# The same steps of an attention and feed-forward kernel in another written-out order, with other engines for some of the elementwise steps

## The chip, the cores and the metric

The kernel runs on one core of a Trainium2 chip. The metric is the device time of one execution in microseconds (us), taken as the median of several runs. The core has five instruction queues that matter here: TensorE (PE; its weight loads are shown apart as PEld), VectorE (DVE), ScalarE (ACT), GpSimd (POOL) and SyncE (SP), which issues most of the DMAs. Each engine works through its own queue in order and waits on semaphores for the others.

## The reference

Two blocks follow each other. The attention maps each row of q and k (4 batches, 4 heads, 1088 positions, 32 dimensions) to 64 features, products of two sketches of 8, and then applies the linear form of attention. Its output is laid out as 4352 tokens of 128 numbers and goes through a multiplicative feed-forward network with 1024 inner features.

```python
def phi(x):
    a = np.einsum('rd,bhsd->bhsr', S1, x)
    b = np.einsum('rd,bhsd->bhsr', S2, x)
    return np.einsum('bhsi,bhsj->bhsij', a, b).reshape(*x.shape[:-1], r * r)
q_p, k_p = (phi(q), phi(k))
kv = np.einsum('bhsf,bhsd->bhfd', k_p, v)
z = np.sum(k_p, axis=2)
num = np.einsum('bhsf,bhfd->bhsd', q_p, kv)
den = np.einsum('bhsf,bhf->bhs', q_p, z)[..., None] + 1e-06
x = (num / den)              # transposed to (4352, 128)
h = (x @ w1) * (x @ w2) @ w3
out = h @ w_out
```

The denominator can come near zero, so the kernel computes it with numbers split into a leading part and a rest. The weights and sketches arrive as 64-bit floats and are turned into fp32 on the chip.

## The kernel before, in words

The program is cut into 1179 named steps, each a function that emits the instructions of one small piece of work. A string named ORDER (lines 75 to 143) lists the names, and the loop at line 1892 calls the steps in that order. Lines 1900 to 1904 then chain the instructions of each engine in the order in which they were emitted, so the string fixes every engine's queue.

```python
for name in ORDER.split():
    n = len(traced)
    steps.pop(name)()
```

The names have a prefix for the piece and a suffix for the operation:

- `w0` to `w10`: the weights. `.load` fetches 64-bit words, `.c` and `.m` (ScalarE) and `.j` (VectorE) and `.a` (GpSimd) turn them into fp32 (lines 422 to 504). `f0` to `f7` fold w3 with w_out, so that one product replaces two (`.m`, line 534).
- `k0` to `k3`: the keys of a batch. `.lead` and `.rest` split k into a leading part and a rest (lines 641 to 651), `.gram0` to `.gram4` form the Gram matrix (128*32 tiles of TensorE, line 659), `.Gm`, `.Gt`, `.Ga`, `.Gb`, `.T0`, `.Ta`, `.N0`, `.Na`, `.N1`, `.Nb` are a chain between TensorE and VectorE that turns it into the denominator's matrix (lines 847 to 937), and `.Nh`, `.Nf`, `.Nr` put that into block form (lines 939 to 954). `.kp0` and `.kp1` make the features of k (line 677), `.kv0` to `.kv3` and `.kvr` multiply them with v (line 769), `.kqt` and `.kq` turn the result. `kr0` and `kr1` are the last 64 positions of two batches each.
- `q0` to `q6` and `qr`: tiles of queries. q0 and q1 have 512 positions, q2 and q3 512 in another layout (`q_wide`, line 1309), q4 and q6 1024, qr the rest. `.A0`, `.C0`, `.C1` are their products with the sketches, `.sm` to `.rc` compute the reciprocal of the denominator (`.p01`, `.p2`, `.p12` multiply leading parts and rests), `.phi` makes features, `.pt` or `.pT` transposes them, `.x` multiplies with kv and `.xT` copies the result into the tile that the network reads.
- `g0` to `g3` and `gr`: the network for one tile of tokens. For each of 8 chunks of inner features, `.a` and `.b` are products of 128*128 weights with up to 512 columns (lines 1799 and 1809), `.c` copies a out of PSUM (line 1804), `.m` multiplies it with b (VectorE, line 1815), and `.o` adds the chunk's output (line 1835, for gr `.o0` and `.o1`, line 1824).
- `h4` and `h6`: the same network for two tiles of tokens at a time with seven products instead of eight (Strassen's way, in Winograd's form). Their first products, such as `h4.0a1`, use 64*128 halves of TensorE's array (line 1673), two at a time; the second ones, `P1` to `P7`, 128*64 halves (line 1759). `.m11` and the like multiply (line 1707), `.T1` to `.T4` form sums (lines 1723 to 1742), `.k1` to `.k9` combine the outputs.
- `s`: constants; `v` and `o`: sums of weights for h4 and h6; `warm0` to `warm11`: idle products on zeros (line 255), 53 in all, which keep TensorE at work where it would stand.

Three more constants belong to the order. SLOTS (line 28) names the buffer that each tile takes, in the order of allocation. The set POOL (line 53) lists the steps whose elementwise operation runs on GpSimd instead of VectorE, through `on(name)` at line 176. The set CPV (line 65) lists the copies that run on VectorE instead of ScalarE, through `cp(name)` at line 179. Large loads are also held back so that at most four are under way (line 1898).

TensorE can work with its whole array (128*128) or with a part of its rows or columns (128*32, 128*64, 64*128, 32*32 and so on). In the trace each product shows the shape that it uses.

## Time and profile before

| what | value |
|---|---|
| runs | 245.04, 245.12, 245.30 us |
| median | 245.12 us |
| span of the profiled execution, first to last instruction | 244.1 us |
| TensorE, products | 236.2 us, 97% |
| VectorE | 206.7 us, 85% |
| GpSimd | 161.9 us, 66% |
| ScalarE | 123.5 us, 51% |
| chain that ended last | 87% TensorE, 5% DMA |

The profile shows one execution. Its busy times are unions of the instructions' spans on an engine; the ends of products are modelled, so the starts are what one compares. A row of a group gives the source line, the engine, the operation, the tile written and read, the shape, the count, and then busy time in us, the mean of one in ns, and the idle time ahead of it. A row of the timeline gives the start in us from the first instruction, the duration, and in brackets an idle time ahead of it with what ended it. "Issue" in such a bracket means that the engine waited for nothing that the profile shows. A row of the busy times by stretches gives the stretch, its length, then for each engine the busy time and the number of instructions, then the granted clock of TensorE, the DMA engines' share and GB/s.

### The profile page before, as it was taken

Reading aid. Unit: us, or ns where it says so; the run is one execution under the profiler, and the core shown is the slowest. Engines: PE = TensorE matmul, PEld = TensorE weight load, DVE = VectorE, ACT = ScalarE, POOL = GpSimd, SP = SyncE. Lnnn points to the kernel's source line nnn. Section 1 sums busy time; section 2 is a strip of 40 time slices with the busy share of each in tenths; the row PEclk is TensorE's granted clock in tenths of the full one; section 3 lists DMA queues with packets and bytes.
Section 4 is the critical chain, followed back from the end, with each engine's and each line's share of the span. In section 5 each row is a group of like instructions: output and inputs, shape, how many; then the busy total and the mean of one; then the engine's idle time right before and its main releaser. Section 6 shows DMA issues by size and latency. Waiting matters only on the chain.

```text
span 244.1 us, 6745 instructions
## 1 busy us (share of the span) xinstructions
PE 236.2 (97%) x2724; PEld 129.8 (53%) x2724; DVE 206.7 (85%) x421; ACT 123.5 (51%) x246; POOL 161.9 (66%) x203
## 2 busy tenths in 40 slices
PE   8998999899999999999999999999999999999994
PEld 5887454545545646766566444444443354463363
DVE  2876988999899998997899878498989789999792
ACT  3976957675666764593012914355651164730010
POOL 4576658344856998764583889929999425883670
PEclk9999999999999999999999999999999999999999
DMA  7959797078859897200000000360000000000054
GB/s 201 265 143 325 181 227 190 6 197 224 220 141 251 188 217 190 59 1 3 3 0 0 4 0 3 59 113 3 1 0 0 0 3 0 0 1 3 12 90 93
DMA packets 31935, 22.06 MB, mean 90 GB/s; under 512 B 21280, under 2 KB 26528, under 8 KB 31904
## 3 DMA queue, kind: packets, MB, share of 16 engines
q1 hardware_dynamic: 31360, 21.11, 35.1%
q8 instruction: 21, 0.34, 0.6%
q10 hardware_dynamic: 544, 0.52, 0.6%
q14 instruction: 10, 0.08, 0.1%
HBM read 19.40 MB, written 2.23 MB: 89 GB/s over the span
## 4 chain that ended last, share of the span: by engine, by line
PE 87%; DMA 5%; ACT 2%; POOL 2%; DVE 1%; issue 1%; POOLq 0%; SPq 0%
PE b_ps L1809 12%; PE ps_o L1835 12%; PE ps_X L1673 11%; PE a_ps L1799 11%; PE ps_o L1759 10%; PE ps_w3o L534 6%; PE ps_Y L1673 6%; PE ps_Z L1673 3%; PE ps_g L659 2%; PE ps_x L1527 2%; PE ps_ac L1374 2%; DMA qh<-in_q_dram 2%; DMA k<-in_k_dram 2%; PE ps_or L1824 2%; POOL ph L1208 1%; PE idle_ps L255 1%
## 5 line engine op out<-in xcount | busy, mean ns | idle before, releaser
L1673 PE MATMUL ps_X<-xd,wv 64*128 64x512 f32 x112 | 36.3, 593 | 0.0
L1799 PE MATMUL a_ps<-xT,w 128*128 128x512 f32 (+1 forms) x80 | 36.1, 562 | 0.0
L1809 PE MATMUL b_ps<-xT,w 128*128 128x512 f32 (+1 forms) x80 | 35.6, 555 | 0.0
L1804 ACT COPY ffa<-a_ps 128x512 f32<-128x512 f32 (+1 forms) x38 | 20.1, 540 | 29.2 <-PE a_ps L1799 26.7
L1707 POOL TENSOR_TENSOR hc<-hc 128x512 f32<-128x512 f32 x16 | 20.7, 1304 | 15.7 <-DVE hc L1685 15.5
L1835 PE MATMUL ps_o<-ab,w3o 128*128 128x512 f32 x64 | 29.6, 600 | 0.0
L1680 ACT COPY hc<-ps_X 128x512 f32<-128x512 f32 x38 | 21.3, 590 | 16.1 <-PE ps_X L1673 12.9
L1815 DVE TENSOR_TENSOR ab<-ffa,b_ps 128x512 f32<-128x512 f32 (+1 forms) x40 | 23.9, 623 | 4.9 <-PE b_ps L1809 4.1
L501 POOL TENSOR_TENSOR w3c<-w3c,cv_m 128x512 int32<-128x512 int32 x16 | 21.2, 1344 | 4.2 <-DVE w3c L495 4.1
L1673 PEld LDWEIGHTS ps_X<-xd,wv 64*128 64x128 f32 x112 | 14.9, 186 | 13.1 <-issue 10.9
L1799 PEld LDWEIGHTS a_ps<-xT,w 128*128 128x128 f32 x80 | 14.1, 189 | 13.9 <-issue 8.8
L1809 PEld LDWEIGHTS b_ps<-xT,w 128*128 128x128 f32 x80 | 14.4, 190 | 13.1 <-issue 8.1
L1673 PE MATMUL ps_Y<-xd,wv 64*128 64x512 f32 x48 | 19.7, 594 | 0.0
L1835 PEld LDWEIGHTS ps_o<-ab,w3o 128*128 128x128 f32 x64 | 11.6, 190 | 13.4 <-issue 13.0
L534 PEld LDWEIGHTS ps_w3o<-wo,w3T 128*128 128x128 f32 x128 | 15.3, 192 | 2.4 <-issue 2.4
L534 PE MATMUL ps_w3o<-wo,w3T 128*128 128x128 f32 x128 | 15.7, 276 | 0.0
L1759 PE MATMUL ps_o<-hc,w3o 128*64 128x512 f32 x32 | 15.1, 595 | 0.0
L1759 PE MATMUL ps_o<-tt,ws 128*64 128x512 f32 x32 | 13.7, 594 | 0.0
L1680 ACT COPY hc<-ps_Y 128x512 f32<-128x512 f32 x14 | 8.1, 592 | 9.7 <-PE ps_Y L1673 6.6
L263 ACT ACTIVATE cv_c<-raw 128x1024 f32<-128x1024 f32 (+1 forms) x13 | 13.0, 1014 | 0.0
L1540 ACT COPY xd<-ps_x 64x256 f32<-64x256 f32 x24 | 8.8, 367 | 7.2 <-PE ps_o L1835 6.8
L1497 POOL COPY nz<-nz 32x8 f32<-32x8 f32 x32 | 11.1, 347 | 1.4
(347 smaller groups left out, 593.0 us busy)
## 6 DMA issues: line engine op xcount, KB each, us to landing
raw<-in_moe_w_dram SPq DMA_DIRECT2D x32, 256.0 KB, 5.0
qh<-in_q_dram SPq DMA_DIRECT2D x4, 544.0 KB, 4.5
raw<-in_moe_w_dram SPq DMA_DIRECT2D x4, 512.0 KB, 5.8
out_dram<-oT SPq DMA_DIRECT2D x32, 64.0 KB, 2.0
k<-in_k_dram SPq DMA_DIRECT2D x3, 512.0 KB, 5.1
v<-in_v_dram SPq DMA_DIRECT2D x2, 512.0 KB, 6.1
kh<-in_k_dram SPq DMA_DIRECT2D x8, 128.0 KB, 3.6
raw<-in_moe_w_out_dram SPq DMA_DIRECT2D x4, 256.0 KB, 5.0
```

Source lines behind the costliest of these rows:

```text
L263: act.activation(dst, hi.bitcast(F32), ACT.Prelu, scale=2.0 ** -112, alpha=-2.0 ** 32)
L501: pool.tensor_tensor(d, d, x["m"][:, i * 512:(i + 1) * 512], ALU.add)
L534: pe.matmul(t["o"], w3T[ko][:, c], wo[:, c], start=c == 0, stop=c == NC - 1)
L1673: pe.matmul(x[bank], stat(j, u)[:, i * 128:(i + 1) * 128], rows(j, u), start=new, stop=True, tile_position=(u * 64, 0), skip_group_check=True)
L1680: cp(n(y))(x[k], x[bank])
L1707: on(f"h{g}.{i}m{k}").tensor_mul(both[0][k], both[0][k], both[1][k])
L1759: pe.matmul(acc_o[bank][half[0]:half[1]], w(i), x(i), start=n == 1, stop=n == (2 if j == 3 else 4), tile_position=(0, half[0]), skip_group ...
L1799: pe.matmul(x["a"][:, :w], w_of(0, c), xT[g][:, c0:c0 + w], start=True, stop=True)
L1804: cp(f"g{g}.{c}{su}c")(x["s"][:, :w], x["a"][:, :w])
L1809: pe.matmul(x["b"][:, :w], w_of(1, c), xT[g][:, c0:c0 + w], start=True, stop=True)
L1815: dve.tensor_mul(ab_sb[g, c][:, c0:c0 + w], x["s"][:, :w], x["b"][:, :w])
L1835: pe.matmul(o_ps[g], w3o[:, c], ab_sb[g, c], start=n == 1, stop=n == NC)
```

## The change

No function is changed and no instruction is added or taken out. The first 61 names of ORDER stay; the other 1118 are put into another order, SLOTS is rewritten to go with it, and POOL and CPV have other members. 33 steps leave POOL and 33 others enter it. Of those that leave CPV, seven are real copies (for `k2.kT1`, `k3.kT0` and `k3.kT1` the set has no effect, since their transposes always run on VectorE); 21 enter it. Parts of the diff:

```diff
 POOL = set("""
-    g4.oS g5.oS g6.oS g7.oS h4.0T1 h4.0T2 h4.0T3 h4.0m12 h4.0m22 h4.1T2 h4.1m11 h4.1m12 h4.2m11
-    h4.2m12 h4.2m22 h4.3m11 h4.s2 h4.s4 h6.0T2 h6.0m11 h6.0m12 h6.0m22 h6.1T2 h6.1T3 h6.1m11 h6.1m12
-    h6.1m22 h6.2T1 h6.2T4 h6.2m11 h6.3T3 h6.3m11 h6.s1 h6.s2 h6.s4 k0.Nf k0.Nh k0.Nr k0.kp1 k1.Nr
-    k1.kp1 k2.kp0 k2.kp1 k2.rest0 k3.kp0 k3.kp1 q0.al q0.p01 q0.phi1 q0.sca q1.al q1.bs q1.p12
-    q1.phi q1.sca q2.bs q2.p2 q2.phi0 q2.sc q2.sl q3.al q3.bs q3.p01 q3.p12 q3.p2 q3.phi0 q3.sc
-    q4.al q4.bs q4.nn q4.p01 q4.p2 q4.phi0 q4.sl q6.al q6.nn q6.p01 q6.phi1 q6.sc q6.sl qr.al qr.bs
-    qr.p12 qr.p2 s.KS s.Pp s.blk s.blkh s.low s.rest
+    g4.oS g5.oS g6.oS g7.oS h4.0T1 h4.0T2 h4.0T3 h4.0T4 h4.0m11 h4.0m22 h4.1T1 h4.1T3 h4.1m11
+    h4.1m22 h4.2T2 h4.2T4 h4.2m11 h4.3m11 h4.s2 h4.s3 h4.s4 h6.0T1 h6.0T2 h6.0T3 h6.0T4 h6.0m11
+    h6.0m12 h6.0m22 h6.1T3 h6.1T4 h6.1m12 h6.1m22 h6.2T1 h6.2T3 h6.2m11 h6.2m12 h6.2m22 h6.3m12
+    h6.s2 h6.s3 h6.s4 k0.Nh k1.kp0 k1.kp1 k2.Nr k2.kp0 k2.kp1 k3.kp1 q0.p01 q0.phi0 q0.phi1 q0.sca
+    q1.al q1.p12 q1.p2 q1.phi q1.scy q2.al q2.bs q2.p12 q2.p2 q2.phi0 q3.al q3.bs q3.p01 q3.p2 q3.sc
+    q4.al q4.bs q4.p12 q4.p2 q4.phi0 q4.phi1 q4.sc q4.sl q6.bs q6.p2 q6.phi0 q6.sl qr.al qr.p2
+    qr.phi0 qr.sc s.AR s.KS s.Pp s.blk s.blkh s.low s.rest
 """.split())
 CPV = set("""
-    g0.0c g0.1c h4.1ac h4.1ad h6.1bc h6.2ad k0.kT1 k1.kvc k2.kT1 k2.kq k3.kT0 k3.kT1 k3.kq q0.xc0
-    q0.xc1 q6.xT0 q6.xT2
+    g0.0c g0.1c g0.6c g1.3c g1.5c g2.0c g2.1c g3.0c g3.2c g3.3c g3.6c gr.2c gr.4c h4.0ac h4.1ad
+    h4.1bd h4.2bd h6.0ae h6.2be h6.3bd k0.kT1 k1.kT1 k2.kq k3.kq q4.xT1 q4.xT2 q6.xT2 q6.xT3
 """.split())
```

And the order at its start, around the Gram products of k2, and at its end:

```diff
-k1.zero s.Pm warm5 q0.l1 q0.A0 warm6 kr0.ab k0.lead1 q0.rm q0.sma q0.sta warm7 k0.kT0 v0.load v0.loadr k1.load k0.ab1
-q0.sha k0.rest1 q0.C0 k0.gram1 k0.gram2 k0.gram3 k0.gram4 k0.ab0 k0.abc1 q1.max q0.C0t q0.sla q1.l2 k1.loadr s.Pp
-k0.Gm k0.Gt k0.Ga w1.c1 k0.Gb k0.abc0 k0.T0 q1.l1 warm8 kr0.abc k0.kp1 q0.sca w1.j1 k0.Ta k0.kp0 k0.Gc w1.c0 k1.tr0
-kr1.load k2.zero k1.tr1 k1.kT1 kr0.kp warm9 k0.N0 warm10 k0.Na warm11 k0.T1 k0.kv0 k0.Tc k0.Tb k0.N1 k0.Nb k0.Nh q1.rm
...
-q1.pc0 q1.pt1 g0.1b w9.load k1.N0 s.AR q2.l1 q2.rm v3.zero q1.pc1 k1.N1 q1.x g0.6c g0.1c k1.Na k1.Nr k3.zero k2.gram0
-g0.1m k2.gram1 k2.gram2 q3.max k2.gram3 g0.0c k2.kT0 k1.Nb q1.xT k2.gram4 q3.l2 k2.ab q2.A0 q2.C0 q2.C1 q3.l1 k1.kp0
...
-h6.1P2 h6.3P6 h6.2m12 h6.2T4 h6.3T4 h6.2P7 h6.2P6 h6.3P4 h6.2P4 g4.oT h6.2P2 gr.3o1 h6.k1 gr.2o0 gr.2o1 h6.2P3 h6.k3
-g4.oS h6.k2 h6.k4 h6.0P3 gr.7o0 g4.st gr.0a gr.5b h6.k5 h6.k6 h6.3P3 h6.1P3 h6.k7 g5.oS q6.ns gr.4a gr.3o0 gr.4b gr.0c
...
+k1.zero s.Pm warm5 q0.l1 q0.A0 warm6 kr0.ab k0.lead1 q0.rm q0.sma q0.sta q0.sha k0.ab1 q0.C0 kr1.load k0.gram1 k0.abc1
+k0.rest1 q0.sla v0.loadr s.Pp k0.kT0 k0.ab0 kr1.tr k0.kp1 q1.max v0.load s.KS k1.loadr warm11 k0.gram2 k0.abc0
+k0.gram3 k0.gram4 q0.C0t k0.kp0 kr1.kT k0.kv0 k0.Gm q1.l2 k0.kv3 kr0.abc k1.load k0.kv1 k0.Gt k0.Ga k0.T0 w1.c0 q0.sca
+q0.al k0.Gc k0.Gb k0.Ta q0.phi0 k0.T1 k1.tr1 q1.l1 w0.load k0.N0 k1.max q1.rm kr1.ab w9.load kr0.kp k0.Na k0.Tc q0.pt0
+w1.c1 k0.Nh k0.Tb q0.A1 k1.kT1 q1.load q1.A0 q0.smy q1.sm k0.N1 k0.Nb k0.kv2 q0.sty q1.C0 k0.Nf q0.phi1 k1.lead0 w1.j1
...
+k3.zero k1.Gt k1.Ga q1.de g0.5c k0.kq s.AR g0.4b k2.lead0 g0.7c g0.0a q1.rc k1.Gb k2.rest0 q1.bs k2.kT1 w0.a0 k1.T0
+k2.gram0 k1.T1 k1.Ta k2.gram1 k2.gram2 q2.max k2.gram3 k2.gram4 q3.l2 k1.N0 g0.5m g0.4m g0.0c g0.3a k2.Gm g0.2c q1.phi
+w9.j w9.m g0.7b q3.l1 q1.pt1 k1.Tc k1.Tb q1.pt0 g0.7m q2.l2 g0.1a k3.loadr w2.load k3.load k1.kp0 q1.pc0 k1.Na v1.zero
+s.RC v1.load k1.Nr g0.1b g0.6m g0.1c g0.1m q1.pc1 k1.N1 g0.3c q1.x q2.l1 q1.restT k2.ab k1.Nb q2.A0 q1.xT q2.rm q2.C0
...
+h6.2P1 h6.3P5 h6.2T3 h6.1P2 gr.2m h6.3P3 q6.ns h6.3T4 h6.3P2 h6.k1 h6.2P7 h6.3P6 h6.1P5 h6.2P6 h6.3P7 h6.1P3 h6.k2
+h6.k3 h6.2P4 h6.3P4 h6.k4 h6.k5 h6.k7 h6.k6 h6.0P3 h6.k8 gr.2o1 g6.oT gr.0a gr.0c gr.4b gr.3a gr.2o0 gr.6b gr.5b h6.k9
+gr.7o1 gr.4m g4.oS g7.oT gr.3c gr.0b g6.oS gr.1o0 gr.1o1 gr.5m gr.4o1 gr.4o0 gr.7o0 g4.st gr.0m gr.6m gr.3b g7.oS
+g6.st gr.3m gr.5o0 gr.0o1 gr.0o0 g7.st gr.6o1 gr.3o1 gr.6o0 gr.5o1 gr.3o0 gr.oT0 gr.oT1 gr.st1
```

In the new order warm7, warm8, warm9 and warm10 stand far behind the start: warm9 ahead of `qr.max`, warm8 ahead of `g3.4c`, warm7 ahead of `g0.7o` and warm10 ahead of `g3.1o`.

More of the change, by code (lines that the diff above doesn't have):

```diff
@@ L83 @@
-q0.al k0.Nf q0.phi0 q0.phi1 q0.A1 q0.smy w1.m1 k1.max q0.sty q0.shy k0.kv3 k0.kv1 k0.kv2 q0.sly s.KS k0.kvr kr1.tr
-k0.kvm w1.m0 kr1.kT q0.p01 q1.C0 q1.C1 q0.C1 k0.kzt k2.loadr q0.pt0 q0.C1t q0.scy q0.p2 k0.kz q0.pt1 k0.kvc kr1.ab
-k0.kqt q0.p12 q0.dn q0.de q0.rc w1.j0 q0.pc0 q0.pc1 q0.x0 k1.kT0 q0.x1 q0.xs0 q0.xs1 q0.xt0 w1.a0 q1.A0 k2.load
-w0.load k1.lead0 q0.xc0 q0.xc1 k0.kq w1.a1 k2.max q0.xt1 k1.ab q0.xT0 q0.xT1 g0.4a q1.load g0.5a q1.sm w0.m1 q1.st
-q1.Ct g0.4c g0.4b q1.sh q1.sl k1.rest0 g0.7b w0.c1 g0.7a k1.abt w0.j1 k1.gram0 w0.c0 s.RC q1.scy k1.gram1 kh2.load
@@ new lines @@
+w1.m1 k1.tr0 q0.de k0.kz q0.x0 w1.m0 q0.rc q1.st q0.pc1 q0.xs0 q1.Ct k2.zero q0.xs1 q1.sh q0.xc0 q0.x1 q0.xt0 q1.sl
+k1.kT0 q0.xc1 kr1.abc q0.xT0 q0.xt1 w0.m0 q1.sca q0.xT1 k1.rest0 w1.a0 k0.kqt k2.loadr w1.a1 k2.load w0.m1 k1.ab g0.4a
+w0.c1 g0.6a q1.p01 q1.al g0.4c g0.5b q1.scy g0.5a k1.gram0 g0.6c q2.tr k1.gram1 k1.gram2 k1.abt k1.gram3 q1.p2 q1.p12
+kh2.load w0.c0 w0.j1 w5.load w0.a1 k1.gram4 q1.dn q3.tr k1.Gm w9.c g0.7a k1.Gc g0.6b g0.2a k2.kT0 k2.max w0.j0 q3.max
+k3.zero k1.Gt k1.Ga q1.de g0.5c k0.kq s.AR g0.4b k2.lead0 g0.7c g0.0a q1.rc k1.Gb k2.rest0 q1.bs k2.kT1 w0.a0 k1.T0
```

122 lines of the change are left out of this document (59 added, 63 removed).

## The prediction

> **What bounds the kernel now.** I read the page first: busy shares, then the busy time by stretches, then the timeline of TensorE around its few gaps.
>
> ```profile
> span 244.1 us, 6745 instructions
> PE 236.2 (97%) x2724; PEld 129.8 (53%) x2724; DVE 206.7 (85%) x421; ACT 123.5 (51%) x246; POOL 161.9 (66%) x203
> ```
>
> ```profile
> 9.50:27.40 17.90, 16.25 (x446) 13.33 (x446) 13.67 (x44) 14.26 (x32) 11.76 (x19) 1.00 0.75 231
> 27.40:156.10 128.70, 127.30 (x1822) 70.92 (x1822) 113.64 (x243) 71.31 (x138) 90.14 (x84) 1.00 0.43 107
> 156.10:240.50 84.40, 84.40 (x400) 39.33 (x396) 74.82 (x121) 33.03 (x63) 56.56 (x69) 1.00 0.14 23
> 242.50:244.10 1.60, 0.00 (x0) 0.00 (x0) 0.00 (x0) 0.00 (x0) 0.00 (x0) 0.71 0.08 27
> ```
>
> In these rows stand the stretch, its length, and the busy time of PE, PEld, DVE, ACT and POOL, then the granted clock. From 27.4 us, where the first large product g0.4a starts, TensorE is busy for 127.3 of 128.7 us, and from 156.1 us without a break. So the time after 27.4 us is what TensorE has to execute, and only three things in it can move: the cost of a change of tile shape, the gaps of about 1.4 us, and the extra instructions that the order puts there. Before 27.4 us TensorE is padded with idle products (warm steps), and the chain through VectorE, ScalarE and GpSimd sets the pace.
>
> The span is 244.1 us and the median of the runs 245.12, so 1.0 us lies outside the span; I keep it as it is and make the sum on the span. About 0.2% (0.5 us) is what a measurement can tell from no change.
>
> **Cost of a change of shape.** One fp32 product is two passes of 512 columns.
>
> ```profile
> 57.02 0.59 PE L1809 MATMUL b_ps<-xT,w 128*128 128x512 f32 x1
> 57.45 1.02 PE L1799 MATMUL a_ps<-xT,w 128*128 128x512 f32 x2
> 58.40 1.10 PE L769 MATMUL ps_kv<-kp,v 128*32 128x64 f32 x64
> ...
> 59.77 1.12 PE L1799 MATMUL a_ps<-xT,w 128*128 128x512 f32 x2
> 60.74 0.59 PE L1809 MATMUL b_ps<-xT,w 128*128 128x512 f32 x1
> ```
>
> By the starts, a pass takes 0.43 us (57.02 to 57.45). The two passes before the change to 128*32 take 0.95 instead of 0.86, so leaving costs 0.09. The two after the return to 128*128 take 0.97, so entering costs another 0.11.
>
> I gave each TensorE step of the two orders its shape from the trace and counted neighbours that differ: 75 in the old order, 64 in the new. Up to g0.4a it is 22 against 18, from there to the first h4 product 42 against 39 (entries into the full array 16 against 14), from there to the end 11 against 7.
>
> ```profile
> 230.33 0.59 PE L1759 MATMUL ps_o<-tt,w3o 128*64 128x512 f32 x1
> ...
> 230.86 0.94 PE L1824 MATMUL ps_or<-w3o,ab 128*128 128x128 f32 x6
> 231.72 1.08 PE L1759 MATMUL ps_o<-hc,ws 128*64 128x512 f32 x4
> 232.73 0.49 PE L1824 MATMUL ps_or<-w3o,ab 128*128 128x128 f32 x2
> 233.06 0.60 PE L1799 MATMUL a_ps<-xT,w 128*128 128x256 f32 x2
> ...
> 234.01 1.08 PE L1759 MATMUL ps_o<-hc,ws 128*64 128x512 f32 x4
> 235.02 0.70 PE L1799 MATMUL a_ps<-xT,w 128*128 128x256 f32 x2
> ```
>
> The four changes that go at the end are two islands of P3 products among the remainder's (231.72 and 234.01); the new order joins them to the long run of P products. From 230.86 to 235.02 pass 4.16 us. The passes alone need 6 x 0.11, twice 0.86 for the islands (four passes on two halves of the array, two at a time), 2 x 0.11 and 0.86 for 0a and 5b: 3.46. That is 0.70 for four changes: **-0.7 us**. In the middle, three fewer at 0.09 and two entries fewer at 0.11: **-0.5 us**. The four at the start I count at nothing: they lie beside the chain that sets the first 27 us.
>
> **The gaps.** Three times the weight loads stop while nothing of the profile holds them.
>
> ```profile
> 14.27 0.11 PEld L659 LDWEIGHTS ps_g<-k,kk 128*32 128x32 f32 x1 [0.54 <-issue]
> ```
>
> ```profile
> 20.35 0.15 PEld L769 LDWEIGHTS ps_kv<-kp,v 128*32 128x32 f32 x7 [1.06 <-issue]
> ```
>
> ```profile
> 46.99 0.11 PEld L659 LDWEIGHTS ps_g<-k,kk 128*32 128x32 f32 x1 [1.27 <-issue]
> ```
>
> ```profile
> 0.00:14.26 14.26, 12.59 (x221) 10.28 (x221) 7.93 (x24) 9.53 (x24) 7.66 (x41) 1.00 0.84 236
> 0.00:20.34 20.34, 17.76 (x345) 14.54 (x346) 12.71 (x41) 14.02 (x34) 11.78 (x48) 1.00 0.76 221
> 0.00:46.98 46.98, 42.66 (x850) 29.05 (x851) 35.30 (x101) 33.89 (x75) 27.38 (x66) 1.00 0.73 199
> ```
>
> Products and loads before each stop sum to 442, 691 and 1701: 249 apart, then four times 252. I take this for blocks of instructions that arrive by DMA, one of which isn't there when TensorE runs through the last too quickly. In the old order the block that ends at 1701 is nearly all Gram products of k2 (four steps of 64 instructions). In the new order count 1701 falls in k1.N1, and the same block holds g0.3a, g0.7b, g0.1a and g0.1b, four products of two passes, 3.4 us in which nothing new is needed, against the 1.27 us that was missing. The stop goes: **-1.3 us** (bounds -1.3, and 0 if another block of the stage stops instead; each later block of the new order up to the last h6 product holds several large products or more). The two early stops are in the next part. Also
>
> ```profile
> 38.37 0.66 PE L1246 MATMUL ps_ph<-ident,ph 128*128 128x128 f32 x4 [0.24 <-POOL ph L1208]
> ```
>
> goes, since q1.pt1 and q1.pt0 move behind g0.3a and g0.7b: **-0.2 us** (bounds -0.2 and 0).
>
> **Warm steps.** warm7, 8, 9 and 10, six idle products, leave the start. They stand now between the large products of the middle, where TensorE has no idle time.
>
> ```profile
> 10.03 0.61 PE L255 MATMUL idle_ps<-zeros 128*128 128x256 bf16 x4
> 10.47 0.26 PE L1038 MATMUL ps_a<-Rh,q 128*128 128x32 bf16 x4
> ```
>
> Four take 0.44 us, so six cost **+0.65 us** there. What they free at the start is no gain while the chain paces it.
>
> **The start, to g0.4a.** VectorE now makes both kp products of k0 (k0.kp1 comes from GpSimd) ahead of the Gram's maximum k0.Gm.
>
> ```profile
> 14.91 0.19 DVE L217 TENSOR_REDUCE G_g<-ps_g 128x1 f32<-128x32 f32 x1 [1.35 <-PE ps_g L659]
> ...
> 16.63 1.21 DVE L677 TENSOR_TENSOR kp<-kab 128x1024 f32<-128x1024 f32 x1
> 17.76 0.15 DVE L217 TENSOR_REDUCE N_g<-ps_N 128x1 f32<-128x8 f32 x1
> ```
>
> ```profile
> 19.20 0.67 POOL L949 TENSOR_TENSOR RS<-RC,mask 128x64 f32<-128x64 f32 x1
> ```
>
> ```profile
> 22.52 0.29 PE L1030 MATMUL ps_cy<-q,RS 128*32 128x128 f32 x4
> ```
>
> k0.Gm waits behind up to 1.21 us of kp work, with T0, N0, N1 and the rest of the chain on TensorE behind it. But one kp product no longer stands between Ta and Na (16.63), and Nf (0.67 us on GpSimd) goes to VectorE. C1, which needs Nf, starts at 22.52 though Nf had ended at 19.87, so 2.6 us of lateness disappear there. Against that, the block boundary at count 691 now falls in k0.N1, on the chain itself, and the last stop there cost 1.06. Bounds: -0.5 (both early stops, 0.54 and 1.06, go, and a third of it reaches the end) and +1.6 (one kp product and a part of a stop). I take **+0.4 us**, nearer to the slack of 2.6. The loads that change places on SyncE's queue (kr1, ahead of v0; w9 ahead of q1, k2 and kh2) are each used several microseconds after their issue by the list, so nothing is charged.
>
> **New waits.** k2.rest0 goes from GpSimd to VectorE and stands close ahead of k2.gram0.
>
> ```profile
> L651 DVE TENSOR_TENSOR kk<-k,kk 128x1152 f32<-128x1152 f32 x2 | 2.7, 1348 | 0.0
> L651 POOL TENSOR_TENSOR kk<-k,kk 128x1152 f32<-128x1152 f32 x1 | 2.6, 2625 | 0.9 <-DVE kk L214 0.9
> ```
>
> It halves the step, but puts 1.35 us into VectorE's queue. Five large products cover it between k1's last Gram and k2's first (4.3 us): **+0.2 us**, bounds 0 and 1.35. At the end:
>
> ```profile
> 230.18 0.68 DVE L1779 TENSOR_TENSOR oc<-oc,ps_o 64x512 f32<-64x512 f32 x1 [1.08 <-PE ps_o L1759]
> 230.97 0.68 DVE L1776 TENSOR_TENSOR oc<-oc,ps_o 64x512 f32<-64x512 f32 x1
> ...
> 237.28 1.90 DVE L1815 TENSOR_TENSOR ab<-ffa,b_ps 128x256 f32<-128x256 f32 x5
> ```
>
> From the first sum of h6 (k3, 230.18) VectorE works without a break to 239.18, 9.0 us for eight sums, two transposes and five multiplications. In the new order the same items but k2 follow the P6 products: 8.3 us, then gr.3o1, 6o0, 5o1 and 3o0 (four times 0.22) must wait for gr.3m: 9.5 us from the last P6 with 0.3 of handing over. TensorE's own work from there is 2.15 us of P products and 6.5 of the remainder's, 8.8 with a change. The excess is 0.7; I take **+0.5 us**, bounds 0 and 1.0.
>
> **Sum.** -0.7 - 0.5 - 1.3 - 0.2 + 0.65 + 0.4 + 0.2 + 0.5 = -0.95. I say -1.0 on the span: 243.1, and 244.1 us for the run.
>
> **The rivals.** *VectorE becomes the bound of the middle (slower).* 33 steps go from GpSimd to VectorE and 33 back, but 21 copies go from ScalarE to VectorE and only seven return. By durations of the same shapes VectorE gains about 8 us, some 5.5 of them between 27.4 and 156.1, where it now idles for 15.1 us (128.70 - 113.64). For it speaks that copies and multiplications of g0 to g3 free the banks that TensorE writes next; against it, that ten microseconds of idle time remain. It decides once the waits for VectorE ahead of TensorE in that stretch exceed 1.0 us. If half of the 5.5 us comes through, -1.0 + 2.75 gives 246.9; chance 0.17.
>
> *No new waits (faster by more).* The start keeps its time, and the waits at k2.gram0 and at the end do not occur: -2.7 + 0.65 = -2.05, 243.1 us; chance 0.20. For it: the old order, with VectorE nearly as full, shows hardly a wait of TensorE after 47 us.
>
> *The gain is eaten (no change).* The early stop at count 691 costs its whole 1.06 on the chain and the end its 1.0: -0.95 + 0.65 + 0.5 = +0.2, 245.3 us; chance 0.18.
>
> *The clock drops in the start.* With four warm steps gone, TensorE stands longer between its steps there. The rows show full clock up to 242.5, 1.9 us after the last product, and 0.71 on average after that. If a gap of over 2 us halved the clock for 3 us, 1.5 us of work would be lost: 245.6 us; chance 0.03, since the gaps I expect there are below 2 us. The Trainium skill, "TensorE: Matmul & The Clock Gate", in "Why this matters for your kernels", warns of the same: no idle gap of TensorE above some 3 us, or the clock falls to half; the last row agrees in direction, and the rule speaks against taking warm steps from the start.
>
> That the order does not have fewer changes is excluded by the count.
>
> **How the numbers follow.** Forecast -1.0 (between -0.5 and -1.6): 0.42. With the rival of a greater gain, faster has 0.62; no change 0.18; slower 0.17 + 0.03 = 0.20. The faster cases alone reach from 242.3 (2.05 and the -0.5 of the start, with rounding) to 244.6. For 8 in 10 the range goes from 242.2 to 246.2, which leaves out the worse half of the slower case and the last tenth of the greater gain.
>
> **What would show it.** Right: no issue gap at the Gram products of k2; P3 products of h6 within the run of P products and no islands after it; g0.4a at 27.4 to 28.2; 0.5 us or so of waiting for VectorE near gr.3o1; idle products of 0.11 between the large ones of the middle. Wrong: g0.4a after 29; over 1 us of TensorE's waiting for VectorE between 28 and 156; a stop of the loads at another count; a clock under 1.00 before 240.

## The result and the profile after

The changed kernel takes 257.19 us (median of four runs, 256.56 to 259.41) against 245.21 for the kernel before beside it (four runs, 245.04 to 245.30). The ratio is 1.0505, with a 95% interval of 1.0457 to 1.0553: slower by 5%. The prediction said 244.1, faster. Here and below a run over 1.5% above the fastest of its kernel counts as slow, and the ratios leave it out, while the medians include it. The profiled execution took 257.75 us, 1.85 of them outside its span.

The head of the page after has the span and the busy time of the engines:

```profile
span 255.9 us, 6771 instructions
PE 240.7 (94%) x2724; PEld 140.2 (55%) x2724; DVE 224.2 (88%) x441; ACT 112.2 (44%) x226; POOL 162.3 (63%) x203
```

TensorE has the same 2724 products, but 4.5 us more of busy time, and its share falls from 97 to 94%. VectorE has 17.5 us more, twice what the prediction had worked out. The span is 11.8 us longer, and three fixed points split it: the start of g0.4a (27.42 before, 31.43 after), the first product of h4 (155.71 and 163.03), and the end of the last product (240.56 and 251.54). First the kernel before, then the one after, in busy times by stretches:

```profile
27.42:155.71 128.29, 126.89 (x1819) 70.60 (x1819) 113.33 (x242) 71.29 (x138) 89.73 (x84) 1.00 0.43 107
155.71:240.56 84.85, 84.85 (x401) 39.63 (x400) 75.11 (x121) 33.03 (x63) 56.95 (x69) 1.00 0.14 24
```

```profile
9.50:20.00 10.50, 9.48 (x287) 8.27 (x286) 9.76 (x28) 9.35 (x21) 7.70 (x13) 1.00 1.06 284
20.00:27.40 7.40, 5.50 (x112) 4.51 (x112) 3.56 (x15) 4.24 (x10) 1.45 (x4) 0.77 0.66 153
...
31.43:163.03 131.60, 126.90 (x1824) 70.25 (x1824) 122.90 (x249) 57.99 (x110) 77.07 (x74) 1.00 0.38 96
163.03:251.54 88.51, 88.26 (x405) 49.65 (x400) 79.67 (x128) 32.78 (x65) 70.00 (x80) 1.00 0.11 19
```

So the start gives +4.0 us, the middle 131.60 - 128.29 = +3.3, the last part 88.51 - 84.85 = +3.7, and the time after the last product +0.8 (3.54 before, 4.36 after). In the middle TensorE's busy time is the same (126.9): there the loss is waiting. In the last part it is busy nearly throughout, with longer products. In the start the granted clock falls to 0.77 on average, and the DMA engines are full ahead of that (1.06).

**The start.** The timeline of TensorE, and then the busy times by single microseconds:

```profile
19.66 0.23 PE L912 MATMUL ps_Nr<-T_p,P2b 32*32 32x8 f32 x5
21.86 0.22 PE L912 MATMUL ps_Nr<-T_p,P2b 32*32 32x8 f32 x2 [1.97 <-issue]
```

```profile
21.00:22.00 1.00, 0.14 (x11) 0.14 (x14) 0.00 (x0) 0.36 (x1) 0.00 (x0) 0.80 1.09 240
22.00:23.00 1.00, 1.00 (x43) 0.96 (x43) 0.61 (x4) 0.00 (x0) 0.00 (x0) 0.50 0.90 245
...
24.00:25.00 1.00, 1.00 (x28) 0.95 (x24) 0.00 (x0) 0.51 (x3) 0.49 (x2) 0.50 0.24 82
25.00:26.00 1.00, 1.00 (x28) 0.80 (x21) 0.68 (x3) 1.00 (x4) 0.00 (x0) 0.99 0.04 9
```

TensorE stops for 1.97 us in the middle of k0.N1, on the chain, with nothing named that holds it. By the trace 692 products and weight loads had started (691 at the 0.91 us stop of products in the old order's k0.kv3). With TensorE's semaphore and drain instructions it is 705 in both; counted so, the old order's three stops come at 449, 705 and 1729 instructions, 256 and four times 256 apart. A 16 KB transfer of the instruction queue goes from 19.07 to 20.37 us (before, from 16.75 to 18.94), and TensorE goes on 1.49 us after it has landed (1.41 before). In all ten traces with a stop at this count, of 0.33 to 2.80 us, that time is 1.38 to 1.52 us: the stop is long or short by when the transfer lands. The clock is at half from 21.60 to 25.02 us, 3.2 us of it after the stop, which costs about 1.6. In a run below with the same order up to here, where the stop happened to last 0.33 us and the clock stayed at 1.00, g0.4a starts at 27.87. So the new order of the chain itself costs 27.87 - 27.42 = +0.45, and the stop and the clock the other 3.6.

**The middle.** The view of TensorE's waits, its first five groups (us in total, times, longest):

```profile
PE ps_ac L1374 <- DVE q L1352: 2.7, 1, 2.7
PE ps_Nr L912 <- issue: 2.0, 1, 2.0
PE ps_xs L1287 <- ACT xs L1280: 1.0, 1, 1.0
PE idle_ps L255 <- DVE zeros L229: 1.0, 1, 1.0
PE ps_w3o L534 <- ACT ffa L1804: 0.9, 1, 0.9
```

The only stop without a named cause is the one in the start: the stop of k2's Gram products is gone. The first row is q2.C1 waiting for q2.rm. VectorE and GpSimd around it after, and the same instruction of VectorE before:

```profile
49.60 0.16 DVE L937 TENSOR_TENSOR RC<-RC,ps_N 128x8 f32<-128x8 f32 x1
49.68 3.55 DVE L1352 SCALAR_TENSOR_TENSOR q<-q,qT 128x512 f32<-128x512 bf16 x1
```

```profile
48.28 1.94 POOL L677 TENSOR_TENSOR kp<-kabt 128x1024 f32<-128x1024 f32 x1
50.19 2.48 POOL L501 TENSOR_TENSOR w3c<-w3c,cv_m 128x512 int32<-128x512 int32 x2
```

```profile
43.09 0.68 DVE L1352 SCALAR_TENSOR_TENSOR q<-q,qT 128x512 f32<-128x512 bf16 x1
```

q2.rm reads two operands from SBUF. It takes 0.68 us alone and 3.55 here, from the middle of k1.kp1 to just behind w9.a1 and w9.a0, three GpSimd instructions back to back. The last part has a pair that shows the condition:

```profile
218.01 0.68 DVE L1712 TENSOR_TENSOR hc<-hc,ps_X 128x512 f32<-128x512 f32 x1
...
219.20 1.81 DVE L1707 TENSOR_TENSOR hc<-hc 128x512 f32<-128x512 f32 x1
```

```profile
217.97 4.17 POOL L1707 TENSOR_TENSOR hc<-hc 128x512 f32<-128x512 f32 x3
```

GpSimd multiplies throughout. The VectorE instruction with one input from PSUM takes 0.68, the one with both from SBUF 1.81. Counting every VectorE instruction that is over 0.15 us longer than the shortest of its kind, the old order has 15 with 9.3 us in excess, the new one 24 with 18.7; all 39 ran beside a GpSimd instruction. That is 9.4 of VectorE's 17.5 extra us; the other 8 are the moved work that the prediction had counted. The Trainium skill, "SBUF — State Buffer", "Who interferes with whom", says that a VectorE instruction with two SBUF inputs contends with a GpSimd instruction that reads SBUF, and that the port pair they share is an exclusive lock; the 0.68 and 1.81 agree.

I took each TensorE step's time from its start to the next one's and subtracted the shortest for its kind and 0.1 for a change of shape. In the middle the excess goes from 5.9 to 8.9 us: k2's stop takes 1.4 away, q1.pt0's wait 0.35, q2.C1 adds 3.0, f6.m 1.2 (behind ScalarE, whose w3.c had waited for a load), and the tail of q6's chain 1.1:

```profile
159.88 0.38 PE L255 MATMUL idle_ps<-zeros 128*128 128x256 bf16 x2 [0.43 <-DVE oT L1842]
...
161.61 1.49 PE L1527 MATMUL ps_x<-pT,kq 32*32 32x256 f32 x64 [0.49 <-DVE oT L1842]
```

VectorE works from 157.85 to 161.55 without a break on q6.pT0, g1.oT, q6.pT1 and g0.oT. warm10 starts when g1.oT has emptied a bank, q6.x when g0.oT has. q6.x is the last thing before h4, and its copies are still being made when h4's first products run: h4.1b1 and h4.0b1 are 0.43 and 0.54 late.

**The last part and the end.** The steps are the same and their shortest times sum to the same 81.67 us, but the excess is 5.75 instead of 1.69, less 0.4 for four changes of shape that are gone: +3.7. Six gaps of 0.42 to 0.54 (the two above, and ahead of gr.1a, gr.4a, h6.0P2 and gr.4o1) are 2.7 of it, the rest is spread over products that are 0.1 late. One thing about this part differs between the two traces throughout. The steps of h4 and h6 use one half of TensorE's array each. In the old order all 336 of their products start in pairs, each within 0.03 us of one on the other half; in the new order only 156 do, and 170 are over 0.05 us away from any. The weight loads, as many as before, keep PEld busy for 49.65 instead of 39.63 us (the stretches above). So the two halves run out of step. Whether that makes the loss or only goes with it isn't shown. The P3 products did join the run of P products, up to the change to the remainder:

```profile
243.65 0.59 PE L1759 MATMUL ps_o<-tt,w3o 128*64 128x512 f32 x1
244.17 0.49 PE L1824 MATMUL ps_or<-w3o,ab 128*128 128x128 f32 x2
```

After the last product, the last store (L1562) waits on SyncE's queue behind the stores of g4 to g7, before (first) and after:

```profile
236.40 4.19 SPq L1556 DMA_DIRECT2D out_dram<-oT  x8
240.95 0.62 SPq L1562 DMA_DIRECT2D out_dram<-oT  x1
```

```profile
248.51 4.15 SPq L1556 DMA_DIRECT2D out_dram<-oT  x8
252.77 0.62 SPq L1562 DMA_DIRECT2D out_dram<-oT  x1
```

Before, the stores are issued by 240.59, in time for the last copy (240.60 + 0.29). After, the last copy ends at 251.58 + 0.27 = 251.85 and the queue is free at 252.66. Those are the +0.8.

### The profile page after: what moved, and what is told of

Read it like the earlier page. It is cut to its first block, busy times and chain, and to the rows that moved or that the text cites. A ratio compares the mean times of both kernels' runs of the same rounds, so it can differ in the third digit from the quotient of the medians.

```text
span 255.9 us, 6771 instructions
## 1 busy us (share of the span) xinstructions
PE 240.7 (94%) x2724; PEld 140.2 (55%) x2724; DVE 224.2 (88%) x441; ACT 112.2 (44%) x226; POOL 162.3 (63%) x203
## 4 chain that ended last, share of the span: by engine, by line
PE 71%; DVE 16%; DMA 5%; ACT 3%; issue 2%; SPq 1%; POOL 0%; DVEq 0%
PE ps_X L1673 11%; PE ps_o L1759 10%; PE b_ps L1809 7%; PE a_ps L1799 7%; PE ps_o L1835 7%; PE ps_w3o L534 6%; PE ps_Y L1673 6%; PE ps_Z L1673 3%; DMA raw<-in_moe_w_dram 2%; PE ps_ac L1374 2%; PE ps_x L1527 2%; DVE ab L1815 2%; DMA k<-in_k_dram 2%; PE ps_g L659 2%; DVE pT L1517 2%
## 5 line engine op out<-in xcount | busy, mean ns | idle before, releaser
L1673 PE MATMUL ps_X<-xd,wv 64*128 64x512 f32 x112 | 40.7, 598 | 0.0
L1835 PE MATMUL ps_o<-ab,w3o 128*128 128x512 f32 x64 | 28.9, 594 | 0.0
L501 POOL TENSOR_TENSOR w3c<-w3c,cv_m 128x512 int32<-128x512 int32 x16 | 20.4, 1286 | 13.0 <-ACT cv_m L484 8.1
L1680 ACT COPY hc<-ps_X 128x512 f32<-128x512 f32 x37 | 20.4, 590 | 16.5 <-PE ps_X L1673 15.4
L1804 ACT COPY ffa<-a_ps 128x512 f32<-128x512 f32 (+1 forms) x27 | 14.1, 537 | 25.0 <-PE a_ps L1799 25.0
L1673 PEld LDWEIGHTS ps_X<-xd,wv 64*128 64x128 f32 x112 | 17.7, 186 | 9.3 <-issue 6.3
L1759 PE MATMUL ps_o<-hc,ws 128*64 128x512 f32 x32 | 15.4, 596 | 0.0
L538 ACT COPY w3o<-ps_w3o 128x128 f32<-128x128 f32 x8 | 1.9, 268 | 30.5 <-PE ps_w3o L534 30.5
L1509 POOL TENSOR_TENSOR ph<-s_al,s_bs 128x1024 f32<-128x1024 f32 (+1 forms) x5 | 9.8, 1976 | 7.3 <-DVE s_bs L1490 5.2
L1497 POOL COPY nz<-nz 32x8 f32<-32x8 f32 x32 | 12.5, 389 | 1.4
```

What stands on the lines that cost most here:

```text
L501: pool.tensor_tensor(d, d, x["m"][:, i * 512:(i + 1) * 512], ALU.add)
L1673: pe.matmul(x[bank], stat(j, u)[:, i * 128:(i + 1) * 128], rows(j, u), start=new, stop=True, tile_position=(u * 64, 0), skip_group_check=True)
L1680: cp(n(y))(x[k], x[bank])
L1759: pe.matmul(acc_o[bank][half[0]:half[1]], w(i), x(i), start=n == 1, stop=n == (2 if j == 3 else 4), tile_position=(0, half[0]), skip_group ...
L1804: cp(f"g{g}.{c}{su}c")(x["s"][:, :w], x["a"][:, :w])
L1835: pe.matmul(o_ps[g], w3o[:, c], ab_sb[g, c], start=n == 1, stop=n == NC)
```

## The experiments

The theory: VectorE is held up beside GpSimd at places on the path, q2.rm above all, and the start stops for a block of instructions that comes late behind loads, after which the clock falls. The rivals: VectorE simply has too much work (the 21 copies); the warm steps are missing; the order of the half products in the last part. Line numbers in the experiments are one or two below those of the kernels shown.

**The warm steps back.** warm7 to warm10 return to the start.

```diff
+q0.sta warm7 ... q1.l1 warm8 ... warm9 k0.N0 ... warm10 k0.Na
...
-w6.a1 warm9 ... q6.C1 warm8 ... g3.5m warm7 ... g0.oT warm10
```

> The kernel after with its four idle steps (warm7 to warm10, 6 products) put back to the start, at the places that they have in the kernel before. In the kernel after, TensorE stops for 1.97 us in k0.N1 (19.89 to 21.86) and the granted clock is then 0.50 for about 3.2 us (21.8 to 25.0). Theory that the idle products keep the clock: the stop stays near 2 us, the clock stays at 1.00, and the time falls by 1 to 2 us, to about 255.5. Rival, that the stop alone drops the clock whatever runs ahead of it: the stop and the half clock stay, and the time stays within 0.7 us of 257.2.

Measured: 256.93 us, ratio 1.0474 (1.0431 to 1.0517), the same as the change. The stop comes at q1.A0 and lasts 1.42 us, and the clock falls all the same:

```profile
23.00:24.00 1.00, 1.00 (x32) 1.00 (x28) 0.72 (x3) 0.24 (x2) 0.43 (x1) 0.50 0.93 284
24.00:25.00 1.00, 1.00 (x27) 0.96 (x20) 0.35 (x2) 1.00 (x5) 0.50 (x2) 0.50 0.45 173
```

The missing idle products are not the cause of the stop or of the clock.

**w9.a1 and w9.a0 later.**

```diff
-q3.st w9.a1 ... g1.3c w9.a0
...
+q2.p2 w9.a1 ... q2.p12 w9.a0
```

> The kernel after with w9.a1 and w9.a0 (GpSimd) later, behind q2.p2 and q2.p12. In the kernel after, q2.rm on VectorE takes 3.55 us (0.68 in the kernel before) while GpSimd works without a break on k1.kp1, w9.a1 and w9.a0, and TensorE waits 2.70 us for q2.C1. Theory that the two engines shut each other out and q2.rm has to wait until GpSimd pauses: q2.rm falls to about 1.2 us, since k1.kp1 alone is left over it, the wait for q2.C1 to under 0.6 us, and the time by 2.0 to 2.7 us, to about 254.8. Rival, that VectorE is the bound of the middle: the wait comes back at other places behind it, and the time stays above 256.5.

Measured: 252.62 us, ratio 1.0298 (1.0276 to 1.032). VectorE, then TensorE:

```profile
48.48 1.10 DVE L1351 SCALAR_TENSOR_TENSOR q<-q,qT 128x512 f32<-128x512 bf16 x1
```

```profile
49.73 0.51 PE L1373 MATMUL ps_ac<-q,RC 32*32 32x128 f32 x32 [0.27 <-DVE q L1351]
```

q2.rm is held up by one instruction only, and the wait falls from 2.70 to 0.27. Of the 2.43 us 0.86 come back as a longer wait ahead of q2.x (1.05). Another 1.2 us of the gain belong to the start, whose stop was 0.91 in this run (g0.4a 30.22). This split is of the profiled execution, the slowest of the kernel's runs at 254.94 us, with a span 2.7 us shorter than the change's; the rest of the 4.6 us by the medians it can't place. The hold-up is shown as the cause of this wait.

**Old start, new rest; new front, old end.** The first kernel takes the 181 steps up to g0.4a in the old order with the old engines, the second the last 435 steps. The buffers had to be dealt out anew.

```diff
-ORDER: first 181 steps of the kernel after
+ORDER: first 181 steps of the kernel before, with their POOL and CPV
```

> The kernel after with the first 181 steps, up to g0.4a, in the order and on the engines of the kernel before, the other steps in the order of the kernel after. Theory that the start costs 4.0 us by itself (g0.4a at 31.43 against 27.42): g0.4a at 27.4, the clock 1.00 throughout, and a time of about 253.2. Rival, that the later stretches swallow it, because loads and VectorE are then late instead: over 255.

```diff
-ORDER: last 435 steps of the kernel after
+ORDER: last 435 steps of the kernel before, with their POOL and CPV
```

> The kernel after with the last 435 steps, from the first products of h4 on, in the order and on the engines of the kernel before. Theory that the last part costs by itself (83.9 us of TensorE from h4.0a1 to the last product before, 88.5 after, and 0.8 us more behind it): the time falls by 4 to 5.4 us, to about 252.5. Rival, that the part is slow because of what is left undone ahead of it (VectorE's backlog at 158 us): it falls by less than 2 us.

Measured: 260.2 us, ratio 1.06 (1.0552 to 1.0649), and 261.17, ratio 1.064 (1.06 to 1.068). With the old start g0.4a begins at 27.11 at full clock, so 4.3 us were won there, but seven new waits of 0.4 to 1.4 us follow (k1.N0 1.32, f2.m 1.42, k2.kv0 1.34, q2.C0 1.04 among them). With the old end the start stops for 2.80 us and h4.0a1 waits 3.28 us for VectorE; the clock is at half for 3.41 us at the first and for 6.83 behind the second. Since slots and neighbours changed as well, neither run prices its part of the change. They show that a part doesn't keep its cost under other surroundings.

**The sets without the order, and the order without the sets.** The new order with the old POOL and CPV, the old order with the new ones, and the new order with the old ones for h4, h6 and gr alone.

```diff
-POOL, CPV: members of the kernel after
+POOL, CPV: members of the kernel before
```

> The kernel after with the sets POOL and CPV of the kernel before: its order and its slots, but every elementwise step on the engine that it had before. Theory that the loss behind the start comes from the engines chosen (VectorE is busy for 17.5 us more, of which some 10 are instructions that stand beside GpSimd's and take longer than the shortest of their kind): VectorE falls back to about 207 us, and the time by 4 us or more, to 253 or less. Rival, that the loss comes from the order: within 1.5 us of 257.2, or slower, as GpSimd's steps then stand at places that weren't chosen for them.

```diff
-POOL, CPV: members of the kernel before
+POOL, CPV: members of the kernel after
```

> The other way round: the kernel before, its order and slots, with the sets POOL and CPV of the kernel after. By the theory of the engines VectorE rises to 214 to 224 us and the time to 249 or more. By the theory of the order it stays under 246.5.

```diff
-POOL, CPV: members of the kernel after
+POOL, CPV: h4.*, h6.* and gr.* as in the kernel before
```

> The kernel after with the sets of the kernel before for the steps of h4, h6 and gr alone. If the engines chosen there make the last part slow (88.5 us of TensorE from h4.0a1 to the last product, 83.9 before), it falls by 3 us or more, and the time to about 254. If it is VectorE's backlog from the part ahead, or the order, by less than 1 us.

Measured: 283.05 us, ratio 1.1434 (1.1337 to 1.153); 282.79, ratio 1.145 (1.1369 to 1.1531); 268.63, ratio 1.0973 (1.0918 to 1.1028). Either half alone costs about 35 us by the ratios, nearly three times the whole change, with VectorE's busy time at 217.1 in the first and 226.4 in the second. The third costs 11.4 us on top of the change. So it isn't the amount of VectorE's work that decides; an order and its engines belong together. In the third the start is the clean one quoted above (27.87).

**The load w0 held back in the start.** Its first DMA waits for k0.Ta, and everything behind it on SyncE's queue with it.

```diff
+HOLD = {"w0.load": "k0.Ta"}
...
+    for load, gate in HOLD.items():
+        ins = next(i for i in made[load] if i.engine == nc.sync.engine)
+        tc.add_manual_dep(ins, made[gate][-1].name, landed, reason="held")
```

> The kernel after, where the first DMA of w0.load waits for k0.Ta (17.9 us) instead of going out at 11.4 us; those behind it on SyncE follow. The DMA engines are busy without a break from 11 to 22 us in the kernel after, and the block of TensorE's instructions that ends the stop in k0.N1 arrives at 19.07 to 20.37 us (16.75 to 18.94 in the kernel before, with the stop of 0.91). Theory that the block queues behind the loads: it arrives about 2 us earlier, the stop is under 1 us, the clock stays at 1.00, and g0.4a starts 1.5 to 2.5 us earlier than 31.4. Rival, that the stop hangs on where the block ends and not on the loads: it stays between 1.4 and 2.8 us, the clock falls to 0.50 as it did, and g0.4a stays at 30.2 or later.

Measured: 260.17 us, ratio 1.0599 (1.0558 to 1.0641). The busy times of the start:

```profile
9.50:20.00 10.50, 9.60 (x284) 8.28 (x283) 9.20 (x26) 9.22 (x22) 7.21 (x13) 1.00 0.53 131
20.00:28.77 8.77, 6.89 (x166) 4.73 (x162) 8.36 (x26) 8.31 (x19) 5.80 (x7) 1.00 0.98 258
```

The DMA share ahead of 20 us is 0.53 instead of 1.06, the instruction transfer starts at 16.25, k0.N1 has no stop, the clock stays at 1.00 and g0.4a begins at 28.77, 2.7 us earlier. So this stop and the half clock behind it hang on the loads that are issued there; 1.35 us against the old order's 27.42 remain. The total got worse: loads are later, up to 54 us TensorE waits 1.04 at k2.gram0, 1.32 at k1.N0, 0.78 at k2.ab and 1.03 at q2.C0, and from 54.30 to 57.72 the clock is at half.

**Copies back to ScalarE.** Eight of the last part, then these and nine of the middle.

```diff
-CPV: ... gr.2c gr.4c h4.0ac h4.1bd h4.2bd h6.0ae h6.2be h6.3bd
```

> The kernel after with eight copies of the last part (gr.2c, gr.4c, h4.0ac, h4.1bd, h4.2bd, h6.0ae, h6.2be, h6.3bd) on ScalarE again, where the kernel before has them, and nothing else changed. ScalarE is busy for 11 of 24 us and 2 of 12.5 us there, VectorE for 22.4 and 12.5. Theory that VectorE bounds the last part: the time falls by 1.5 us or more. Rival, that the order makes the waits there (products placed ahead of what frees their banks): it stays within 0.7 us, net of what the stop in k0.N1 does from run to run.

```diff
-CPV: ... the same eight, g0.6c g1.3c g1.5c g2.0c g2.1c g3.0c g3.2c g3.3c g3.6c
```

> The kernel after with these eight and nine copies of g0 to g3 (g0.6c, g1.3c, g1.5c, g2.0c, g2.1c, g3.0c, g3.2c, g3.3c, g3.6c) on ScalarE again; some 11 us less work for VectorE. Theory that VectorE bounds the kernel behind the start: a fall by 3 us or more, to 254 or less. Rival, that single instructions held up beside GpSimd do it and not the amount of work: the waits at q2.C1 (2.70), f6.m (0.88) and q6.x (0.49) stay, and the time falls by less than 1.5 us.

Measured: 257.38 us, ratio 1.0498 (1.0456 to 1.054), and 258.05, ratio 1.0427 (1.0386 to 1.0469). With 17 copies fewer the page has for VectorE, and the view of waits for q2.C1:

```profile
PE 240.8 (95%) x2724; PEld 143.4 (56%) x2724; DVE 215.4 (85%) x424; ACT 120.7 (47%) x243; POOL 162.1 (64%) x203
```

```profile
PE ps_ac L1372 <- DVE q L1350: 2.7, 1, 2.7
```

8.8 us of work leave VectorE and none of the middle's waits does: 2.71 at q2.C1, 0.93 at f6.m, 0.48 at q6.x; the hold-ups are still 25 with 18.6 us. The rival "too much work" falls: by the ratios the 17 copies gain 2 us at most, and their interval overlaps the change's; the eight gain nothing. The gaps ahead of gr.4a and h6.0P2 vanish in both kernels, but they also vanish or shrink where w9's load is moved and no copy (the next experiment), so the copies aren't shown to be their cause. That the total hardly moves although both starts are 2.7 us shorter (g0.4a 28.66 and 28.70, stops of 0.92 and 0.88, clock 1.00) is in part the clock again: behind the gap at q2.C1 it is at half for 3.41 us with 17 copies and 6.83 with eight, which the profiled run of the change did not have.

**w9's load later**, behind kh2's; and this with w9.a1 and w9.a0 later and the 17 copies on ScalarE.

```diff
-kr1.ab w9.load
...
+kh2.load w9.load
```

> The kernel after with w9.load (four DMAs of 256 KB, out at 14.4 to 19.3 us) behind kh2.load on SyncE, as the kernel before has it behind kh2. It sheds DMA traffic at the time when the block of instructions for k0.N1 is fetched, and holds nothing else up. Theory that this block queues behind the loads: the stop in k0.N1 (0.3 to 2.8 us in five runs of the same start) falls under 0.5 us, the clock stays at 1.00, g0.4a starts at about 28, and the time falls by 1 to 3 us. Rival, that the fetch is slow anyway: the stop stays over 0.9 us and the clock falls.

```diff
-kr1.ab w9.load ... q3.st w9.a1 ... g1.3c w9.a0
...
+kh2.load w9.load ... q2.p2 w9.a1 ... q2.p12 w9.a0
-CPV: ... the 17 copies
```

> Three of the edits on the kernel after together: w9.load behind kh2.load, w9.a1 and w9.a0 later on GpSimd, and the seventeen copies on ScalarE again. If the costs stand at separate places, the gains add: 4.5 (w9.a alone) and 1 to 3 (the loads) and what the copies give, to 246 to 250 us. If VectorE and GpSimd only meet elsewhere, the total stays above 252. Under 244.8 would mean that the order with fewer shape changes is worth having once these are out of the way.

Measured: 259.0 us, ratio 1.0543 (1.0484 to 1.0603), and 256.86, ratio 1.0426 (1.0355 to 1.0498). In the profiled executions the start behaves (g0.4a 27.42 and 27.55, no stop, clock 1.00). But w9.c on ScalarE now waits for its load, and ScalarE's queue stands with it (ScalarE, then TensorE, of the first):

```profile
35.35 1.13 ACT L262 ACTIVATE cv_c<-raw 128x1024 f32<-128x1024 f32 x1 [5.64 <-DMA raw<-in_moe_w_dram]
```

```profile
38.85 1.13 PE L1798 MATMUL a_ps<-xT,w 128*128 128x512 f32 x2 [2.30 <-ACT ffa L1803]
```

g0.0a waits for a copy queued behind w9.c. In the second kernel it waits 2.54 us, and the clock is at half for 3.41 us behind it; together the three changes miss the 246 to 250 us expected of them. A load moved without its consumer gives back what it wins.

**The half products.** Each step of h4 and h6 uses half of TensorE's array, and a half works through its own products, so I put products of both halves side by side where the new order has neighbours on one half (11 steps moved). The reverse in the kernel before: nine swaps that make neighbours use the same half.

```diff
-h4.0b2 h4.s4 h4.0a6 h4.0a3
...
+h4.0b1 h4.0a6 ... h4.1bh h4.s4 h4.0a3
```

> The kernel after with some products of h4 and h6 moved by a few places in ORDER, so that products for the two halves of the array take turns in twos, as they do throughout in the kernel before; slots and engines unchanged. Counted by hand, with each product holding its half for 0.86 us and TensorE taking products strictly in order, the runs of products need 30.0, 22.3 and 12.9 us in the order of the kernel after where 26.6, 20.6 and 12.0 are possible; this edit brings them to 28.3, 20.6 and 12.0. Theory that products of the same half behind each other leave the other half idle: h6.0b6 to gr.4a falls from 21.98 to about 20.8, h6.0P6 to gr.2o1 from 12.89 to about 12.1, and the time by 2 to 4 us. Rival, that VectorE sets the pace of the last part: these stretches stay within 0.4 us of what they were, and the time within 1 us.

```diff
-h4.1bc h4.0b6 ... h4.1bh h4.2b1
...
+h4.0b2 h4.0b6 ... h4.0b4 h4.2b1
```

> The kernel before with nine neighbouring products of h4 and h6 exchanged so that two for the same half of the array stand behind each other at nine places, and nothing else. Theory of the halves: 0.43 us (one pass of one half) to 0.86 us (a whole product) at each, thus 3.9 to 7.7 us more, 249 to 253. Rival, that TensorE fetches products out of order and fills the free half: within 0.5 us of 245.1.

Measured: 257.41 us, ratio 1.0509 (1.0469 to 1.055), no effect (from h6.0P6 to gr.2o1 12.89 us in both, the whole last part 88.87 against 88.51). The swaps in the old order: 248.89 us, ratio 1.0163 (1.0124 to 1.0203), +3.5 us, 0.39 for each. So neighbours on one half do cost. Whether the new order loses there stays open, since the 11 moves didn't bring its halves back into step: 120 of the 336 products start in pairs, against 156 in the change. The old order with the nine swaps looks like the new one: 156 of 336 in pairs, weight loads busy for 47.8 instead of 39.63 us, and the last part 3.35 us longer (88.20 against 84.85).

**All causes at once.** Warm steps in the start, w9's load later and w9.c with it, w9.a1 and w9.a0 later, and the 11 half products; then without the half products but with five copies on ScalarE.

```diff
-kr1.ab w9.load ... k1.Gm w9.c ... q3.st w9.a1 ... g1.3c w9.a0
...
+kh2.load w9.load ... q1.phi w9.c ... q2.p2 w9.a1 ... q2.p12 w9.a0
```

> The kernel after with the causes found so far taken away together: w9.load behind kh2.load (and w9.c later, just ahead of w9.j, so that ScalarE doesn't wait for it), the four idle steps back at the start, w9.a1 and w9.a0 later on GpSimd, and the products of h4 and h6 taking turns as in the run with pairs. If the causes are these and stand apart: 12.1 less 3 to 4 (stop and half clock), 2.4 (q2.rm) and 2 to 4 (halves), thus 247 to 250. Under 244.8 would mean that fewer changes of shape are worth having. Over 252 would mean that a cause is missing.

```diff
-CPV: ... gr.2c gr.4c h6.0ae h6.2be h6.3bd
```

> The kernel after with w9.load behind kh2.load and w9.c ahead of w9.j, the four idle steps at the start, w9.a1 and w9.a0 later, and five copies of h6 and gr (h6.0ae, h6.2be, h6.3bd, gr.2c, gr.4c) on ScalarE again; the products of h4 and h6 in the order of the kernel after. If waits for VectorE cost time in the last part, those ahead of gr.4a and h6.0P2 (0.42 and 0.43 us) go, and the time is about 252.3 (253.3 with the pairing and without these copies moved). If the last part is slow for another reason, it stays at 253.3 or above.

Measured: 253.32 us, ratio 1.0328 (1.0302 to 1.0353), and 251.62, ratio 1.024 (1.0187 to 1.0293). The first was expected at 247 to 250, and over 252 was to mean that a cause is missing: one is. The second is 5.6 us below the change and some 6 above the kernel before. Its page and stretches, of its fastest run (250.66):

```profile
span 248.9 us, 6770 instructions
PE 238.3 (96%) x2724; PEld 138.8 (56%) x2724; DVE 218.5 (88%) x436; ACT 114.9 (46%) x231; POOL 161.8 (65%) x203
```

```profile
28.37:157.07 128.70, 126.30 (x1819) 69.77 (x1819) 120.01 (x249) 58.33 (x110) 77.56 (x74) 1.00 0.43 107
157.07:244.49 87.42, 87.17 (x405) 49.42 (x400) 76.29 (x123) 35.08 (x70) 70.03 (x80) 1.00 0.12 20
```

Start +0.95, middle 128.70 - 128.29 = +0.4, last part 87.42 - 84.85 = +2.6, end +0.9, in all 4.8 us of the span: the start and the middle are all but mended. In the middle 1.05 ahead of q2.x and 1.09 ahead of q6.x remain. The last part keeps h4.1b1, h4.0b1, gr.1a and gr.4o1.

**The P3 products joined in the old order**, so that its shape changes at the end fall by the same four.

```diff
+h6.2P2 h6.2P3 h6.0P3 h6.3P3 h6.1P3
...
-gr.2o1 h6.2P3 ... h6.k4 h6.0P3 ... h6.k6 h6.3P3 h6.1P3
```

> The kernel before with the products h6.2P3, h6.0P3, h6.3P3 and h6.1P3 right behind h6.2P2, so that they run in one stretch of 128*64 products instead of in two islands of their own among the products of gr; six banks are taken in another order, nothing else changes. It is the part of the change that the prediction gave 0.7 us for, alone. If a change of shape costs what the rows of the kernel before gave (0.09 out, 0.11 in, and the second half that an island of two leaves idle), the time falls by 0.4 to 0.7 us, to 244.5 to 244.8. Rival, that the products of gr then come later and the end waits for VectorE by as much: within 0.3 us of 245.2, or slower.

Measured, in 12 runs against 17: 245.37 us against 244.99, ratio 1.0001 (0.9973 to 1.0028), no difference. From h4.0a1 to the last product:

```profile
155.26:238.91 83.65, 83.56 (x398) 39.31 (x394) 74.12 (x120) 33.00 (x63) 55.92 (x68) 1.00 0.13 23
```

The kernel before takes 240.56 - 156.67 = 83.89 there, so four changes are worth 0.24 us, not 0.70. gr.0o1 now waits 0.26 for VectorE.

## Why the prediction was wrong

The sign and the size were wrong. The steps that concerned TensorE's own work held, and those that said that nothing else would be late failed.

- *End, -0.7.* Mis-sized: 0.24 in the old order's own surroundings, and not to be seen in the time. The step laid the whole excess of 4.16 over 3.46 us to the changes.
- *Middle, -0.5.* 39 changes instead of 42, some 0.3 at 0.1 each. Right in kind, and small.
- *The stop at k2's Gram, -1.3, and q1.pt0's wait, -0.2.* Right, both are gone.
- *Warm steps, +0.65.* Right: the shortest times of the middle's steps sum to 118.83 instead of 118.15, +0.68.
- *Start, +0.4.* The chain was right (+0.45). "The loads that change places on SyncE's queue ... nothing is charged" failed. I looked at who uses the loads, not at what travels beside them: with w0 and w9 issued at 11.4 to 19.3 us, the block of instructions came late to the densest piece of the chain. Holding w0 back or moving w9's load took the stop away in all five kernels that did so; it came in eight of the nine that had the change's loads in the start, from 0.33 to 2.80 us. The step had named the boundary at count 691 in k0.N1 and its bound was +1.6; with the half clock on top the start measured +4.0.
- *k2.rest0, +0.2.* No such wait: nothing.
- *The end's VectorE chain, +0.5.* It came out at gr.4o1 (0.42) instead of gr.3o1. What was missed is SyncE: the last store waits behind eight others, +0.8.
- *The rival "VectorE becomes the bound of the middle".* Its condition, waits of over 1.0 us, was met: 2.70 + 0.49 + 0.43 us for VectorE. Its mechanism was wrong. I priced moved work by "durations of the same shapes" and held it against ten microseconds of idle time. Taking 8.8 us of work away changed none of the waits; moving two GpSimd instructions removed the largest. What grew was the time that instructions with two SBUF inputs stand beside GpSimd, and where it fell on the path.
- *The clock rival.* Priced at 1.5 us, which is about what the half clock cost. But I had asked for a gap of over 2 us and expected smaller ones, and blamed the warm steps; it followed a stop of 1.97 us, and with the warm steps back it came again.
- *What the sum lacked altogether:* the last part's +3.7 us. "From there TensorE is busy without a break" was a property of the old order with its own engines and slots, and I carried it over to the new. In the new order TensorE's two halves run out of step there, and its products start late.

The marks named beforehand told it plainly: g0.4a after 29, over 1 us of waiting for VectorE in the middle, a clock under 1.00.

What stays open: 6 us of the mended kernel. Of the last part's 2.6, the late q6 chain and the four gaps are read from the trace and were not removed one by one, and about half is spread over products that are each only slightly late. The likely candidate for these is that the halves of the array are out of step, which no run took away from the new order. The old start and the old end could not be priced alone. The stop in the start ends some 1.4 us after the transfer of instructions has landed; why the transfer starts anywhere from 17.55 to 20.23 us, with the same loads, isn't settled.

## What to carry to other kernels

A hand-written order, the engines of its steps and its buffers are one object: a change of all three can't be priced as a sum of local edits, and here half of it cost nearly three times the whole. On VectorE, count not only the work that moves but the instructions with two SBUF inputs on the critical path that will stand beside a row of GpSimd instructions. Ask of every bulk load that moves forward what else is travelling then, TensorE's own instructions among it.
